# FNet mixing plus a GEGLU feed-forward: where a third seven-product form starts, which hidden block keeps its left sums, and when weights are asked for

## The chip, the cores and the metric

The kernel runs on one core of one Trainium2 chip. The metric is the device time of one execution in microseconds (us). Before the change three runs gave 1032.2, 1033.59 and 1035.08 us; the median is 1033.59 us. The profile comes from one more execution, with a time of its own (see below).

## The reference, cut to what matters

```python
# x: 2048 x 640; w_gate, w_up: 640 x 1728; w_down: 1728 x 640; all fp32
g = sigmoid((x * gate_w).sum(-1, keepdims=True))
a = x @ dft_hid_re ; b = x @ dft_hid_im           # DFT along the hidden side
y = dft_seq_re @ a - dft_seq_im @ b               # DFT along the sequence, real part
h = gelu(x @ w_gate) * (x @ w_up)                 # 2048 x 1728, tanh form
out = g * y + (1 - g) * (h @ w_down)
```

The change lies in the first third of the program, where `h` is computed; its last lines touch the first loads of the DFT.

## The kernel before, in words

**Products.** Every fp32 matrix product is made of three TensorE matmuls on reduced-precision parts: each operand is split into a "high" part (a ScalarE copy with rounding, L82) and a "low" part (the rest, a VectorE subtraction, L85), and `mm3` issues high by high (L101), high by low (L102) and low by high (L103). A low part can also be made without VectorE: `negative` writes minus the high part on ScalarE (L93), and `left_of` adds the raw data onto it with an accumulating DMA that GpSimd issues (L97).

**Seven products.** Large products are cut 2 by 2 and computed with seven block products in place of eight, from sums of blocks. On the weight side these sums are S1 to S4 (VectorE, L311 to L317), a difference D (`diff`, L330), and for pairs of blocks sums "across" the pair. On the side of x they are T1 to T4.

**The loop.** The 1728 columns of `h` are done as 13 blocks of 128 and a rest. Blocks 1 to 12 are the loop `for f in range(1, NF)`. From block `PAIRED` = 3 on, two neighbours form a pair: the odd one (kind 1) carries further seven-product forms over both, `together` (names ending in t: `pH7t`) and `together_up` (u). From block `THIRD` on there is a third such form, `together_s`, for S1 times T1 (s). Its weight operands are called `wt`: raw parts `wt9a`, `wt9b` (loaded by `load_third`, L267), their sums (L277, and L280 to L283 across), highs, and lows. Its x operands `xs` are made once, from blocks read back (`loads_s`), with sums at L1298 to L1303 and splits, kept in DRAM, and read again for each pair by `load_across` (GpSimd's DMA queue, L1329); `xq` and `xu` are the same for the other two forms. An even block (kind 2) of such a pair finds S1 times T1 already in its bank, so its group of S1 is missing, and its group of S4 stands in the place of S1.

**A block's matmuls.** `gate_up` issues, for each half tp of the rows, products into the banks X and Z: A11, S1 (or S4), then S2 (`xT02`, `xT12` with `ws..`), D, S3, S4, and a last small one into X with `u5` (`x05`, `x15` with `wa`). VectorE empties X between them: L637 adds X to a sum after A11 and before S2 may write X, L675 after S3 and before `u5`, L691 after `u5`; L667 takes Z after D in an even block of a pair with `together_s`. In the other blocks S4 into Z stands between S3 and `u5`. ScalarE copies a bank at L149. A matmul that writes X again waits for the one that emptied it. In an odd block L587 empties the bank `pH7s` in `together_s`.

**Left sums.** For the hidden blocks k listed in `STORED` (k counts pairs of f: k=1 is f=3 and 4, k=2 is f=5 and 6), the sums that the later product with `w_down` needs on its left side are made right here (L700 in the odd block, `last_sums` after the even one) and written to DRAM. For the k that is not listed they are made later.

**Order.** Within `in_order` the engines TensorE, ScalarE, VectorE and GpSimd run exactly in the order in which the code issues. The loop interleaves by `fills`, a queue of small pieces with a cost in units of VectorE time: after each group of matmuls `fill(ns)` issues as many pieces as the share of the block's matmul time allows. `make_w(f + 1)` gives the pieces that prepare the next block's weights, `make_third(f + 2)` those of `wt`, `make_up` those of `wu`. Raw weights are asked for on SyncE's queue: `load_w` takes `wa..r` (512 KB), `wb`, and for odd blocks `wq..r`. Tiles of 4 KB per partition share 46 slots, so a load can wait until the last reader of the slot's old tile is done.

**After the loop** the DFT follows: it has its own groups `pL`, `pX`, `pZ`, `pV` from operands `ch`/`cl` (DFT matrix) and `xah`/`xal` (x). Its first x operands, `split_xa(0)` to `split_xa(2)`, are made in block 12. Then come the products with `w_down` in an order of k, and the last sums.

Of the kernel before, what the change touches and what calls it, by code (L numbers as in the profile page):

```python
# [22 lines left out]
NF = F // P  # L23
# [1 line left out]
NK = (NF - 1) // 2  # L25
GM_AT = [5, 19]
EORD = [0, 2, 1, 3, 4]
STORED = (0, 2, 3)
PAIRED = 3
THIRD = 5  # L30
XB_AT = [0, 1, 2, 3, 4, 5, 9, 11]
WU_AT = [17, 19, 33, 35, 50]
HL_AT = [21, 37]
# [4 lines left out]
def kernel(  # L38
# [167 lines left out]
    def pair_of(f):  # L206


        return 0 if f < PAIRED or f >= NF else 2 - (f - PAIRED + 1) % 2
# [3 lines left out]
    def load_w(f):  # L213


        if f >= NF:
            return
        ra, rb = slot(F32, [P, 8, P], f"wa{f}r"), wsmall(F32, f"wb{f}")
        nc.sync.dma_start(ra, wf[f - 1, :, :8])
        nc.sync.dma_start(rb, wf[f - 1, :, 8:])  # L220
        rq = None
        if pair_of(f) == 1:
            rq = slot(F32, [P, 8, P], f"wq{f}r")
            nc.sync.dma_start(rq[:, 0:2], wf[f, :, 0:2])
            nc.sync.dma_start(rq[:, 2], wf[f, :, 4])
        wraw[f] = ra, rb, rq
# [35 lines left out]
    def load_third(f):  # L262

        traw[f] = a, b = [mtile(F32, f"wt{f}{n}").rearrange("p (b c) -> p b c", c=P) for n in "ab"]
        for v, c in ((a, 8), (b, 2)):
            for q in range(2):
                nc.sync.dma_start(v[:, 2 * q : 2 * q + 2], wf[f - q, :, c : c + 2])  # L267
# [30 lines left out]
    def make_w(f):  # L298
# [96 lines left out]
        if kind == 1:  # L395
            if f > PAIRED:
                work = [(0, high_a), (0, neg_a), (84, across), (0, low_a), (56, across2), (0, high_q)]
                work += [(84, sums), (109, low_q), (84, sums2), (0, high_c), (56, diff), (122, low_c)]
            else:
                work = [(84, across), (56, across2), (0, high_a), (0, high_q), (122, low_a), (109, low_q)]  # L400
                work += [(84, sums), (84, sums2), (56, diff)]
                late_work.extend([(0, high_c), (122, low_c)])
        elif kind == 2:
            work = [(84, sums), (28, diff_here), (0, high_a), (84, sums2), (122, low_a), (61, high_c), (0, low_c)]
        else:
            work = [(84, sums), (0, high_a), (84, sums2), (0, high_c), (122, low_a), (56, diff), (122, low_c)]
# [705 lines left out]
    W0, load_part, parts, first_strassen = load_first()  # L1112
    Bs = []
    B, tiles, load, piece, tsum, his, lows = load_x(0)
# [28 lines left out]
    with in_order(ACT, DVE, PE):  # L1143
# [48 lines left out]
        B, tiles, load, piece, tsum, his, lows = load_x(1)  # L1192
# [62 lines left out]
        W, work = make_w(1)  # L1255
        sums, high_a, sums2, high_c, low_a, diff, low_c = (do for _, do in work)
# [70 lines left out]
    def load_across(f, n, to, kept, k):  # L1327
        v = slot(F32R, [P, 2, T], f"{n}{f}{k}")
        nc.gpsimd.dma_start(v.bitcast(F32), kept[k - 1])  # L1329
        to[f"T{k}"] = v[:, 0], v[:, 1]  # L1330

    fills, state = deque(), {}
# [27 lines left out]
    with in_order(PE, ACT, DVE, POOL):  # L1360
        for f in range(1, NF):
# [6 lines left out]
            if kind == 1:  # L1368
                up, work = make_up(f, load_up(f))
# [6 lines left out]
            third = kind == 1 and f >= THIRD  # L1376
            if f + 1 < NF and not third:
                nxt, work = make_w(f + 1)
                if pair_of(f + 1) == 1 and f + 1 >= THIRD:
                    ws, (sums, across, highs, lows) = make_third(f + 1)  # L1380
                    work = [sums, *work[:2], across, *work[2:4], highs, work[4], lows, *work[5:]]
                if kind != 1 or f == PAIRED:
                    fills.extend(work)
            if kind == 1 and PAIRED < f < THIRD:
                fills.extend(work)
            if f == NF - 1:
                for k in range(2):
                    fetch_xn(k)
                    load_c(k)

                def made():
                    sums_made.pop(0)()

                for k in range(2):
                    fills.extend([(126, partial(split_xa, k)), (122, made), (245, partial(split_c, k))])
                fills.extend([(126, partial(split_xa, 2)), (122, made)])
            state.update(pe=0, done=0, all=sum(c for c, _ in fills), pe_all=2450 if not kind else (2994, 1768)[kind - 1] if f < THIRD else (3198, 1496)[kind - 1])
            s5 = pair(F32, f"s5{f}")
            xs = {}
            work = [gate_up(f, W, Bs[tp], tp, s5[:, tp], s1t, xs, s4, zs) for tp in range(2)]  # L1400
# [11 lines left out]
            for k in range(4):  # L1412
                run(more)
                if third and k in (1, 3):
                    load_across(f, "xs", Ts, kepts, k)
            for step in range(8 if not kind else 7):
                if third and step == 5:
                    unpark(f + 1, zs, parks)
# [35 lines left out]
                    fills.extend(s123[:3])  # L1454
                if f == THIRD - 1 and step == 5:
                    todo.extend(s4th)
                if step == 5 and THIRD <= f + 2 < NF and pair_of(f + 2) == 1:
                    load_third(f + 2)
                if third and step == 1:
                    load_w(f + 1)  # L1460
                    nxt, parts = make_w(f + 1)
                    fills.extend(parts)
                    state["all"] += sum(c for c, _ in parts)
                if step == 5 and not (f + 2 >= THIRD and pair_of(f + 2) == 2):
# [461 lines left out]
```

## Time and profile before

| what | us |
|---|---|
| median of three runs | 1033.59 |
| the profiled execution | 1031.1 |
| its span, first to last instruction | 1029.3 |
| TensorE busy / VectorE / ScalarE / GpSimd | 1014.8 / 837.2 / 511.8 / 188.9 |
| loop blocks 3 to 12 (first matmul of block 3 to the first stretch of pure DFT) | about 93 to 360 |

The first matmuls of the blocks, read from the timeline of TensorE, stand at 93.25 (f=3), 123.96, 143.76, 176.13 (f=6), 193.75, 227.53 (f=8), 245.08, 279.21 (f=10), 295.49 and 327.68 us (f=12). In what follows E8 is the first matmul of block 8, and E8+9.8 means 9.8 us behind it.

How to read it: a row of the timeline has start, duration, engine, line, operation, output<-inputs, shapes, and in brackets how long the engine stood idle just before and which instruction released it. A row of the waits has the engine and line that waited, what it waited for, the sum, the number of waits and the longest. TensorE starts matmuls of 512 columns every 0.23 us though each shows as 0.39 us, since they overlap.

### The profile page before, as it was taken

Reading aid. Unit: us, or ns where it says so; the run is one execution under the profiler, and the core shown is the slowest. Engines: PE = TensorE matmul, PEld = TensorE weight load, DVE = VectorE, ACT = ScalarE, POOL = GpSimd, SP = SyncE. Lnnn points to the kernel's source line nnn. Section 1 sums busy time; section 2 is a strip of 40 time slices with the busy share of each in tenths; the row PEclk is TensorE's granted clock in tenths of the full one; section 3 lists DMA queues with packets and bytes.
Section 4 is the critical chain, followed back from the end, with each engine's and each line's share of the span. In section 5 each row is a group of like instructions: output and inputs, shape, how many; then the busy total and the mean of one; then the engine's idle time right before and its main releaser. Section 6 shows DMA issues by size and latency. Waiting matters only on the chain.

```text
span 1029.3 us, 13418 instructions
## 1 busy us (share of the span) xinstructions
PE 1014.8 (99%) x4477; PEld 832.8 (81%) x4477; DVE 837.2 (81%) x1197; ACT 511.8 (50%) x666; POOL 188.9 (18%) x330
## 2 busy tenths in 40 slices
PE   9999999999999999999999999999999999999998
PEld 7888778777778788888888888888888888888887
DVE  7887786868666798986977797779798997997796
ACT  6644455454545484533444444434627737665340
POOL 1221240414130010032104301320111010111112
PEclk9999999999999999999999999999999999999999
DMA  9566684757586897589669966979989999997856
GB/s 350 156 212 225 208 276 176 248 209 254 197 268 228 269 265 225 199 300 388 232 201 341 376 220 218 375 267 325 328 306 384 353 395 335 344 364 216 269 147 98
DMA packets 98598, 276.51 MB, mean 269 GB/s; under 512 B 13088, under 2 KB 25504, under 8 KB 98528
## 3 DMA queue, kind: packets, MB, share of 16 engines
q1 hardware_dynamic: 69216, 182.88, 51.1%
q0 software_dynamic: 29024, 92.57, 28.2%
q8 instruction: 35, 0.57, 0.2%
q14 instruction: 35, 0.29, 0.1%
q10 hardware_dynamic: 288, 0.20, 0.1%
HBM read 201.13 MB, written 66.60 MB: 260 GB/s over the span
## 4 chain that ended last, share of the span: by engine, by line
PE 81%; issue 10%; DVE 4%; POOL 3%; DMA 1%; ACT 0%; POOLq 0%; SPq 0%; DVEq 0%; ACTq 0%
PE pX L102 5%; PE pX L103 5%; PE pX L101 5%; PE pL L103 3%; PE pL L102 3%; PE pL L101 3%; PE pZ L103 3%; PE pZ L101 3%; PE pZ L102 3%; PE pV L103 2%; PE pV L102 2%; PE pV L101 2%; PE pY L103 1%; PE pR L103 1%; PE pQ L103 1%
## 5 line engine op out<-in xcount | busy, mean ns | idle before, releaser
L82 ACT ACTIVATE ch<-csa 128x1024 fp32r<-128x1024 f32 x32 | 34.0, 1063 | 79.6 <-DVE csa L894 66.8
L456 POOL DMA_DIRECT2D hA<-s x48 | 26.2, 546 | 165.8 <-DVE s L687 145.4
L82 ACT ACTIVATE ch<-cra 128x1024 fp32r<-128x1024 f32 x32 | 33.9, 1060 | 45.2 <-DVE cl L85 14.2
L85 DVE TENSOR_TENSOR cl<-cra,ch 128x1024 fp32r<-128x1024 f32 x32 | 39.1, 1221 | 19.7 <-ACT ch L82 16.2
L85 DVE TENSOR_TENSOR cl<-crb,ch 128x1024 fp32r<-128x1024 f32 x32 | 39.1, 1221 | 13.3 <-ACT ch L82 13.1
L102 PE MATMUL pL<-cl,xah 128*128 128x512 f32 x128 | 49.8, 389 | 0.0
L103 PE MATMUL pL<-ch,xal 128*128 128x512 f32 x128 | 49.8, 389 | 0.0
L101 PE MATMUL pL<-ch,xah 128*128 128x512 f32 x128 | 48.7, 389 | 0.0
L82 ACT ACTIVATE ch<-crb 128x1024 fp32r<-128x1024 f32 x32 | 33.8, 1056 | 27.0 <-DVE cl L85 9.7
L85 DVE TENSOR_TENSOR cl<-csa,ch 128x1024 fp32r<-128x1024 f32 x32 | 39.1, 1221 | 9.9 <-ACT ch L82 8.8
L149 ACT ACTIVATE s<-pX 128x512 f32<-128x512 f32 x41 | 24.1, 596 | 37.4 <-PE pX L103 36.8
L85 DVE TENSOR_TENSOR cl<-csb,ch 128x1024 fp32r<-128x1024 f32 x32 | 39.2, 1224 | 4.2 <-ACT ch L82 3.2
L82 ACT ACTIVATE ch<-csb 128x1024 fp32r<-128x1024 f32 x32 | 34.0, 1061 | 12.5 <-DVE csb L897 4.3
L1526 POOL DMA_DIRECT2D uA<-c x8 | 4.3, 540 | 168.5 <-DVE c L1638 168.3
L102 PEld LDWEIGHTS pL<-cl,xah 128*128 128x128 f32 x128 | 24.0, 188 | 5.0
L103 PEld LDWEIGHTS pL<-ch,xal 128*128 128x128 f32 x128 | 24.0, 188 | 5.0
L101 PEld LDWEIGHTS pL<-ch,xah 128*128 128x128 f32 x128 | 24.0, 188 | 5.0
L82 ACT ACTIVATE kh<-kw 128x1024 fp32r<-128x1024 f32 x24 | 25.5, 1062 | 5.1 <-PE kL L102 4.2
L675 DVE TENSOR_TENSOR s<-s,pX 128x512 f32<-128x512 f32 x24 | 16.1, 682 | 13.0 <-PE pX L103 13.0
L102 PE MATMUL pX<-cl,xah 128*128 128x512 f32 x64 | 25.0, 391 | 0.7 <-DVE cl L85 0.7
L85 DVE TENSOR_TENSOR kl<-kw,kh 128x1024 fp32r<-128x1024 f32 x18 | 21.9, 1218 | 4.4 <-ACT kh L82 4.4
L681 ACT ACTIVATE s<-s 128x512 f32<-128x512 f32 x16 | 10.1, 634 | 30.3 <-DVE s L680 30.3
(3785 smaller groups left out, 3524.8 us busy)
## 6 DMA issues: line engine op xcount, KB each, us to landing
cra<-in_ct SPq DMA_DIRECT2D x64, 512.0 KB, 5.1
crb<-in_ct SPq DMA_DIRECT2D x64, 512.0 KB, 5.8
kr<-hA SPq DMA_DIRECT2D x36, 512.0 KB, 7.7
hA<-s POOLq DMA_DIRECT2D x48, 256.0 KB, 3.1
ux<-uA SPq DMA_DIRECT2D x24, 512.0 KB, 8.0
ux<-uT SPq DMA_DIRECT2D x16, 512.0 KB, 6.5
hT<-s POOLq DMA_DIRECT2D x24, 256.0 KB, 5.3
xq<-xp POOLq DMA_DIRECT2D x12, 512.0 KB, 5.3
```

The source lines that it names most:

```text
L82: nc.scalar.activation(hi, raw, AF.Copy)
L85: nc.vector.tensor_tensor(lo, raw, hi.bitcast(F32), op=ALU.subtract)
L101: nc.tensor.matmul(ps, lh, rh, start=first, stop=False, skip_group_check=True)
L102: nc.tensor.matmul(ps, lh, rl, start=False, stop=False, skip_group_check=True)
L103: nc.tensor.matmul(ps, ll, rh, start=False, stop=last, skip_group_check=True)
L149: nc.scalar.activation(m, src, AF.Copy)
L456: nc.gpsimd.dma_start(to[:, i], src)
L675: tt(s5, s5, X, op=ALU.add)
L681: nc.scalar.activation(s2, s2, AF.Gelu_apprx_tanh)
L1526: nc.gpsimd.dma_start(to[:, i], src)
```

## The change

1. `THIRD` goes from 5 to 7: the pair of blocks 5 and 6 computes S1 times T1 in the plain way, and only the pairs 7/8, 9/10 and 11/12 use `together_s`. The sums of `xs` across, which were made in blocks 3 and 4, are made in blocks 5 and 6. TensorE issues 4496 instructions of matmul in place of 4493.
2. `STORED` goes from (0, 2, 3) to (0, 1, 3): the left sums are made at once for blocks 3 and 4 and no longer for 5 and 6. After the loop k=1 and k=2 change places.
3. In an odd block from `THIRD` on, `load_w` of the next block and `load_third` of the next pair are issued after the third step of `together`, where `load_w` stood at step 1 and `load_third` at step 5 of the even block. The pieces of `make_third(f + 2)` move from the even block into the odd one, among the next block's pieces.
4. For odd blocks above 3 the pieces of `make_w` get a new order: the difference D's sum and high part ahead of the high part of the sums S, its low part ahead of the low part of the sums.
5. In block 12 `split_xa(1)` and `split_xa(2)` make their lows by ScalarE's `negative` and the accumulating DMA. Only `split_xa(0)` still uses VectorE's subtraction.

```diff
@@ -25,9 +25,9 @@
 NK = (NF - 1) // 2
 GM_AT = [5, 19]
 EORD = [0, 2, 1, 3, 4]
-STORED = (0, 2, 3)
+STORED = (0, 1, 3)
 PAIRED = 3
-THIRD = 5
+THIRD = 7
 XB_AT = [0, 1, 2, 3, 4, 5, 9, 11]
 WU_AT = [17, 19, 33, 35, 50]
 HL_AT = [21, 37]
@@ -395,7 +395,7 @@
         if kind == 1:
             if f > PAIRED:
                 work = [(0, high_a), (0, neg_a), (84, across), (0, low_a), (56, across2), (0, high_q)]
-                work += [(84, sums), (109, low_q), (84, sums2), (0, high_c), (56, diff), (122, low_c)]
+                work += [(84, sums), (109, low_q), (84, sums2), (28, diff_high), (0, high_c), (28, diff_low), (122, low_c)]
             else:
                 work = [(84, across), (56, across2), (0, high_a), (0, high_q), (122, low_a), (109, low_q)]
                 work += [(84, sums), (84, sums2), (56, diff)]
@@ -1376,7 +1376,7 @@
             third = kind == 1 and f >= THIRD
             if f + 1 < NF and not third:
                 nxt, work = make_w(f + 1)
-                if pair_of(f + 1) == 1 and f + 1 >= THIRD:
+                if f + 1 == THIRD:
                     ws, (sums, across, highs, lows) = make_third(f + 1)
                     work = [sums, *work[:2], across, *work[2:4], highs, work[4], lows, *work[5:]]
                 if kind != 1 or f == PAIRED:
@@ -1392,8 +1392,8 @@
                     sums_made.pop(0)()
 
                 for k in range(2):
-                    fills.extend([(126, partial(split_xa, k)), (122, made), (245, partial(split_c, k))])
-                fills.extend([(126, partial(split_xa, 2)), (122, made)])
+                    fills.extend([(126, partial(split_xa, k, not k)), (122, made), (245, partial(split_c, k))])
+                fills.extend([(126, partial(split_xa, 2, False)), (0, made)])
             state.update(pe=0, done=0, all=sum(c for c, _ in fills), pe_all=2450 if not kind else (2994, 1768)[kind - 1] if f < THIRD else (3198, 1496)[kind - 1])
             s5 = pair(F32, f"s5{f}")
             xs = {}
@@ -1413,6 +1413,10 @@
                 run(more)
                 if third and k in (1, 3):
                     load_across(f, "xs", Ts, kepts, k)
+                if third and k == 2:
+                    load_w(f + 1)
+                    if f + 2 < NF:
+                        load_third(f + 2)
             for step in range(8 if not kind else 7):
                 if third and step == 5:
                     unpark(f + 1, zs, parks)
@@ -1454,11 +1458,13 @@
                     fills.extend(s123[:3])
                 if f == THIRD - 1 and step == 5:
                     todo.extend(s4th)
-                if step == 5 and THIRD <= f + 2 < NF and pair_of(f + 2) == 1:
+                if step == 5 and f + 2 == THIRD:
                     load_third(f + 2)
                 if third and step == 1:
-                    load_w(f + 1)
                     nxt, parts = make_w(f + 1)
+                    if f + 2 < NF:
+                        ws, (sums, across, highs, lows) = make_third(f + 2)
+                        parts = [*parts[:3], sums, across, *parts[3:5], highs, parts[5], lows, *parts[6:]]
                     fills.extend(parts)
                     state["all"] += sum(c for c, _ in parts)
                 if step == 5 and not (f + 2 >= THIRD and pair_of(f + 2) == 2):
```

**Blocks 3 and 4 on VectorE**, from the sums of block 3's last products to the instruction that empties X in block 4 (L637). `s_..` are sums of 512 columns. Before:

```order
L1302 TENSOR_TENSOR xs_1217<-xs_1217,xst_1227 128x512
L1303 TENSOR_TENSOR xs_1219<-xs_1219,xs_1217 128x512
L680 TENSOR_TENSOR s_1_1146<-s_1_1146,pZ_1_1052 128x512
L687 TENSOR_TENSOR s_0_1134<-s_0_1134,s_1001 128x512
L691 TENSOR_TENSOR s_1179<-s_1179,pX_0_1042 128x512
L692 TENSOR_TENSOR s_1033<-s_1033,s_1179 128x512
L687 TENSOR_TENSOR s_1_1146<-s_1_1146,s_1001 128x512
L691 TENSOR_TENSOR s_1196<-s_1196,pX_1_1051 128x512
L692 TENSOR_TENSOR s_1040<-s_1040,s_1196 128x512
L85 TENSOR_TENSOR xs_1297<-xs_1217,xs_1297 128x512
L85 TENSOR_TENSOR xs_1303<-xs_1215,xs_1302 128x512
L637 TENSOR_TENSOR s_1124<-s_1124,pX_0_1289 128x512
```
Now:

```order
L680 TENSOR_TENSOR s_1_1146<-s_1_1146,pZ_1_1052 128x512
L687 TENSOR_TENSOR s_0_1134<-s_0_1134,s_1001 128x512
L691 TENSOR_TENSOR s_1179<-s_1179,pX_0_1042 128x512
L692 TENSOR_TENSOR s_1033<-s_1033,s_1179 128x512
L700 TENSOR_TENSOR s_1001<-s_0_1134,s_1033 128x512
L687 TENSOR_TENSOR s_1_1146<-s_1_1146,s_1001 128x512
L691 TENSOR_TENSOR s_1196<-s_1196,pX_1_1051 128x512
L692 TENSOR_TENSOR s_1040<-s_1040,s_1196 128x512
L700 TENSOR_TENSOR s_1001<-s_1_1146,s_1040 128x512
L637 TENSOR_TENSOR s_1124<-s_1124,pX_0_1266 128x512
```

Four rows on `xs` (L1302, L1303 and two splits, L85) are gone from here, as are three more just ahead of it (L1298, L1299 and a split), and two L700 have come. The seven `xs` rows now stand at the same place of blocks 5 and 6, ahead of block 6's L637.

**Block 7 on VectorE**, around the low part of `wu7` and L587, which empties `pH7s`. `ws8r` are the sums for block 8, `wt9a` and `wt9b` the parts for the third form of block 9. Before:

```order
L85 TENSOR_TENSOR wu7l<-wu7r,wu7h 128x640
L311 TENSOR_TENSOR ws8r<-wb_1977,wa8r 128x256
L312 TENSOR_TENSOR ws8r<-wa8r,wb_1977 128x256
L587 TENSOR_TENSOR sz_1972<-sz_1972,pH7s 128x512
L343 TENSOR_TENSOR wa8r<-wa8r 128x128
L316 TENSOR_TENSOR ws8r<-ws8r,wa8r 128x256
L317 TENSOR_TENSOR ws8r<-wa8r,ws8r 128x256
L596 TENSOR_TENSOR sz_1942<-sz_1942,pH7s 128x512
```
Now:

```order
L85 TENSOR_TENSOR wu7l<-wu7r,wu7h 128x640
L311 TENSOR_TENSOR ws8r<-wb_1874,wa8r 128x256
L312 TENSOR_TENSOR ws8r<-wa8r,wb_1874 128x256
L343 TENSOR_TENSOR wa8r<-wa8r 128x128
L277 TENSOR_TENSOR wt9a<-wt9a,wt9b 128x512
L280 TENSOR_TENSOR wt9b<-wt9a 128x128
L281 TENSOR_TENSOR wt9b<-wt9a 128x128
L282 TENSOR_TENSOR wt9b<-wt9b,wt9a 128x128
L283 TENSOR_TENSOR wt9b<-wt9a,wt9b 128x128
L316 TENSOR_TENSOR ws8r<-ws8r,wa8r 128x256
L317 TENSOR_TENSOR ws8r<-wa8r,ws8r 128x256
L587 TENSOR_TENSOR sz_1956<-sz_1956,pH7s 128x512
```

L343, the five sums of `wt9`, L316 and L317 now stand between `wu7l` and L587; before, only L311 and L312 did. A little ahead of this piece L242 to L245, the sums of `wu7`, now stand in front of L515, L520 and L521; before, they stood behind L521 and L714.

**Block 8 on ScalarE**, where the weights of block 9 get their high parts (`wd` is D, `ws9h` the sums, `wq9h` those across the pair). Before:

```order
L82 ACTIVATE wq9h<-wq9r 128x896
L149 ACTIVATE s_0_2216<-pX_0_2160 128x512
L149 ACTIVATE s_1_2226<-pX_1_2176 128x512
L82 ACTIVATE ws9h<-ws9r 128x1024
L82 ACTIVATE wd_2234<-wb_2118 128x128
L668 ACTIVATE s_0_2216<-s_0_2216 128x512
L671 ACTIVATE s_1967<-s_1967 128x512
```
Now:

```order
L82 ACTIVATE wq9h<-wq9r 128x896
L149 ACTIVATE s_0_2186<-pX_0_2140 128x512
L82 ACTIVATE wd_2194<-wb_2098 128x128
L149 ACTIVATE s_1_2197<-pX_1_2151 128x512
L82 ACTIVATE ws9h<-ws9r 128x1024
L668 ACTIVATE s_0_2186<-s_0_2186 128x512
L671 ACTIVATE s_1951<-s_1951 128x512
```

`wd` has moved from behind `ws9h` to the place between the two copies of X (L149); `ws9h` stays behind the second copy.

## The prediction

> **What bounds the kernel now.** I read the page first, then the waits of TensorE, then the timeline at each of those waits.
>
> ```profile
> PE 1014.8 (99%) x4477; PEld 832.8 (81%) x4477; DVE 837.2 (81%) x1197; ACT 511.8 (50%) x666; POOL 188.9 (18%) x330
> ```
> ```profile
> PE pX L101 <- DVE s L675: 4.4, 3, 1.7
> PE pX L101 <- DVE s L637: 2.2, 3, 1.6
> PE pH9s L101 <- DVE sz L587: 1.6, 1, 1.6
> PE pH7s L101 <- DVE sz L587: 1.3, 1, 1.3
> PE idle L1147 <- PEq L1914: 0.8, 1, 0.8
> PE pX L102 <- DVE cl L85: 0.7, 1, 0.7
> ```
> ```profile
> 360.00:1029.00 669.00, 666.22 (x2965) 550.71 (x2963) 567.72 (x730) 326.60 (x371) 107.50 (x180) 1.00 0.85 287
> ```
>
> TensorE is the bound: 99% busy, clock 1.00. The row of the windows (columns: stretch, length, busy time and count of TensorE, weight loads, VectorE, ScalarE, GpSimd, clock, DMA share, GB/s) shows that behind 360 us it never rests for long: 669 us for 2965 matmuls is 0.226 us each. So a microsecond won in the loop arrives at the end as it is. What there is to win is the list of waits without the idle warm-up row: 4.4+2.2+1.6+1.3+0.7 = 10.2 us in 9 waits. Each is followed by a matmul that takes 0.50 in place of 0.39 us (row 132.48 below), so I count 0.1 more for each: 11.1 us. Every one lies between 124 and 360 us, and every one waits for VectorE.
>
> **The change part by part.** *Extra matmuls.* Three more at 0.226 us: +0.7 us, sure.
>
> *Block 4.* L637 empties X, and S2 waits for it.
>
> ```profile
> 123.56 0.69 DVE L85 TENSOR_TENSOR xs<-xst,xs 128x512 fp32r<-128x512 f32 x1 [1.22 <-ACT xs L82]
> ...
> 130.54 1.28 DVE L85 TENSOR_TENSOR xs<-xs,xs 128x512 fp32r<-128x512 f32 x2
> 131.74 0.68 DVE L637 TENSOR_TENSOR s<-s,pX 128x512 f32<-128x512 f32 x1
> ```
> ```profile
> 132.48 0.50 PE L101 MATMUL pX<-xT02h,ws4h 128*128 128x512 f32 x1 [1.56 <-DVE s L637]
> ```
>
> Ahead of it go seven `xs` instructions at 0.60 us from start to start (two in 130.54 to 131.74), 4.2 us, and the wait of 1.22; two L700 come, at about 0.65: −4.1 us. L637 was 1.6 late, so it is early: the wait is gone: −1.6.
>
> *Block 6* gets these rows in its turn. Its L637 was late by 0.3 (2.2 − 1.56 − 0.3 for block 8). New ahead of it: four of the seven, 2.4 (the other three fall into block 5). Gone: two L700 (1.3) and, since they move behind it, `wt7`'s five sums and three small ones of `wq7`, which is only partly a gain, as VectorE waited there for nothing but its own row. Counted out row by row I get L637 ending 7.7 us behind E6 where TensorE wants it at 6.8: a wait of 1.0. Bounds: 0.3 as it was, 1.6 as in block 4; I take 1.0. On the other hand L675 no longer matters there: with S1 done in the plain way, S4 (twelve matmuls, 2.7 us) stands between S3 and the one that waits, and its 1.7 us go. Sum −1.0.
>
> *Blocks 8 and 10.* The late one is L675:
>
> ```profile
> 237.85 0.60 ACT L149 ACTIVATE s<-pX 128x512 f32<-128x512 f32 x1 [0.67 <-PE pX L103]
> 239.01 1.06 ACT L82 ACTIVATE ws9h<-ws9r 128x1024 fp32r<-128x1024 f32 x1 [0.56 <-DVE ws9r L317]
> ```
> ```profile
> 240.30 0.29 DVE L85 TENSOR_TENSOR wd<-wb,wd 128x128 fp32r<-128x128 f32 x1 [1.12 <-ACT wd L82]
> 240.51 0.68 DVE L667 TENSOR_TENSOR s<-s,pZ 128x512 f32<-128x512 f32 x1
> 241.11 1.22 DVE L85 TENSOR_TENSOR ws9l<-ws9r,ws9h 128x1024 fp32r<-128x1024 f32 x1
> 242.24 0.68 DVE L667 TENSOR_TENSOR s<-s,pZ 128x512 f32<-128x512 f32 x1
> 242.84 1.27 DVE L675 TENSOR_TENSOR s<-s,pX 128x512 f32<-128x512 f32 x2
> ```
> ```profile
> 243.57 0.50 PE L101 MATMUL pX<-x05h,wa 128*128 128x512 f32 x1 [1.68 <-DVE s L675]
> ```
>
> The wait of 1.12 for `wd` goes (ScalarE makes its high part behind `ws9h`, from now on ahead of it), and the sums of the next third form, 2.2 us, have left this block. That would be 3.3 us on VectorE, twice what is missing. But `ws9h` stays behind the second copy on ScalarE, and that copy waits for TensorE (0.67). So now ScalarE sets the time: the copy at 237.4 (0.4 sooner, as L637's waits in this block go), `ws9h` from 238.0 to 239.0, `ws9l` to 240.2, two L667 to 241.4, L675 to 242.0, where TensorE wants it at 241.3 (243.57 less the 1.68 and the slow matmul gives 241.7, less 0.4). A wait of 0.7 stays (bounds 0 and 1.7). So −1.0 here, −0.3 for L637, and −0.3 in block 10, whose wait was 1.0 (4.4 − 1.7 − 1.7) and is limited in the same way.
>
> *Blocks 7 and 9.*
>
> ```profile
> 210.28 0.82 DVE L85 TENSOR_TENSOR wu7l<-wu7r,wu7h 128x640 fp32r<-128x640 f32 x1 [3.07 <-ACT wu7h L82]
> 213.71 0.43 DVE L311 TENSOR_TENSOR ws8r<-wb,wa8r 128x256 f32<-128x256 f32 x1 [2.60 <-DMA wa8r<-in_wf]
> ...
> 214.38 0.68 DVE L587 TENSOR_TENSOR sz<-sz,pH7s 128x512 f32<-128x512 f32 x1
> ```
>
> In block 7 the raw weights come late; asked for at the block's start they end the wait of 2.60. In exchange L343, the five sums of `wt9`, L316 and L317 go ahead of L587: 0.2 + 0.6 + 4 × 0.2 + 0.8 = 2.4 us. And the sums of `wu7` now stand ahead of three instructions of 0.60 us (L515, L520, L521), which fill part of the wait of 3.07 for `wu7h`: I put `wu7l` 1.2 us sooner. L587 then comes 2.6 + 1.2 − 2.4 = 1.4 sooner, and it was 1.3 late; since two of the three are estimates I count 0.3 left (bounds 0 and 1.3). In block 9 the third form's sums fall behind L587, so its 1.6 goes whole. Sum −2.6.
>
> *Block 12.* The two lows leave VectorE for ScalarE and an accumulating DMA.
>
> ```profile
> 339.19 1.06 ACT L82 ACTIVATE xah<-xn 128x1024 fp32r<-128x1024 f32 x1 [3.92 <-DVE xn L860]
> ```
> ```profile
> L93 ACT ACTIVATE xal<-xn x5: 1042/1044/1048, 358.5 to 380.7; 128x1024 fp32r<-128x1024 f32 x5
> L97 POOL DMA_DIRECT2D xal<-xn x5: 857/874/895, 360.0 to 382.2; - x5
> ...
> DMA to landing us min/median/max: 6.1/7.3/9.3
> ```
> ```profile
> 346.32 0.39 PE L103 MATMUL pX<-ch,xal 128*128 128x512 f32 x1
> ```
> ```profile
> 359.05 0.50 PE L102 MATMUL pX<-cl,xah 128*128 128x512 f32 x1 [0.73 <-DVE cl L85]
> ```
>
> The negative starts at 340.2, the DMA 1.5 us later (358.5 to 360.0) at 341.6, and lands by the row at 347.7 to 350.9. TensorE read this low at 346.32; its order now puts the reading five matmuls later, at 347.4. At the lower end the wait is 0.3, at the median 1.5, at the upper end 3.5. DMA is less busy there than at the rows' own time, so I take 0.4. The second low, by the order alone, is asked for some 7 us before TensorE reads it: hidden by the two lower landings, late by 2.3 by the upper; I take 0. In return VectorE is free of two lows of 1.2 us and their waits, and the 0.7 at 359.05 shrinks to 0.2. Sum −0.1.
>
> The sums of k=1 and the swap of k behind the loop I cost at nothing:
>
> ```profile
> 144.00:176.00 32.00, 32.00 (x141) 26.10 (x140) 18.86 (x34) 16.83 (x30) 4.92 (x10) 1.00 0.59 209
> ...
> 194.00:227.50 33.50, 32.20 (x141) 26.18 (x140) 20.57 (x36) 15.81 (x27) 8.14 (x16) 1.00 0.73 251
> ```
>
> In block 5 (first row) VectorE has 13 of 32 us free and TensorE waits for nothing. Six sums and the three `xs` rows fit there; without that cover the six are 3.6 us.
>
> **Sum:** +0.7 −1.6 −1.0 −1.0 −0.3 −0.3 −2.6 −0.1 = −6.2, and with six waits in place of nine three slow matmuls fewer, −0.3: **−6.5 us**, 1024.6 against the profiled 1031.1. The median of the three runs is 2.5 above the profiled one, so the same gain reads 1027 there; I predict 1025.5, between.
>
> **A rule that speaks against it.** The earlier loads (1 MB: `wa` 512 KB and the raw third form 512 KB) run beside the reading of `xs`:
>
> ```profile
> 199.95 1.18 POOL L1329 DMA_DIRECT2D xs<-xs  x2 [1.02 <-DMA xs<-xs]
> ```
> ```profile
> DMA to landing us min/median/max: 6.3/6.6/6.9
> ```
> ```profile
> 206.75 0.39 PE L101 MATMUL pZ<-xs,wt7h 128*128 128x512 f32 x1
> ```
> ```profile
> 299.78 0.33 SPq L219 DMA_DIRECT2D wa12r<-in_wf  x1
> ```
> ```profile
> DMA to landing us min/median/max: 6.6/6.9/7.1
> ```
>
> The first landing line belongs to the two rows of block 7, with no weights beside them, the last to those of block 11 at 299.5, with `wa12r` beside them: 0.3 us longer. The Trainium skill, DMA: Bandwidth & Descriptors, section Issuing engines are not separate DMA queues, says that transfers of all issuing engines share the same 16 DMA engines and interleave. By that rule 1 MB ahead would cost `xs` all of its own time; the two landing lines show little of it.
>
> **Rivals.** *Waits that only move* (15%): L587 with more ahead of it stays at 1.3, block 6 takes 1.6, blocks 8 and 10 keep 1.7 and 1.0. That is 1.0 + 0.6 + 1.3 = 2.9 more: 1028.4. For it: each place is an order written out, with margins under 1 us. Against: the 2.60 and 1.12 are waits for a load and a copy that plainly move.
>
> *The loads come no sooner* (10%): `wa8r` needs a slot, whose last reader is a late matmul of block 6. If VectorE still gets it only at 213.7, the 2.4 us put ahead of L587 come on top: 1.3 grows to 3.7 in block 7 (0.3 counted), and block 9 keeps its 1.6. That is 5.0 more: 1030.5.
>
> *Transfers come late* (8%, slower): `xs` at 199.95 lands at 206.3 and is read at 206.75, a margin of 0.5; in block 9 I put it at 0.5 too, an estimate, once the stalls ahead are gone. 1 MB at block 7's 251 GB/s is 4.2 us; all of it ahead of `xs` costs 3.7 twice, and `xal` landing at 9.3 costs 3.1 more than I count: 10.5 more, or 1036. It decides at `xs` landings of 8.5 us with `xal` at 9.3: then 3.1 and twice 1.7 eat the gain of 6.5; at 10.1 it is slower by more than 3.1. Against: 7.1 was the longest `xs` beside a weight load.
>
> **How the numbers follow.** Forecast 67%, rivals 15, 10 and 8%. Bounds: all waits gone (3.3 counted as left, and six slow matmuls) gives 1021.6, a little less with the small gaps that the view of the waits leaves out; the second rival at the median's level 1033. Range 1020.5 to 1033.5. A difference under 0.3% (3.1 us) can't be told from none: faster takes the forecast and most of the first rival, 0.79; same the second and the rest, 0.13; slower 0.08.
>
> **What would show it.** Right: no wait for L637 in block 4 but one in block 6 near 1.0; no `DVE ws8r <- DMA wa8r` among VectorE's waits; L675 twice near 0.7, behind `ws9h`; no wait of `pH9s` for L587; 4496 matmuls' worth of work. Wrong: TensorE waiting for a DMA of `xs`, `xq` or `xal`, or for L587 with more than 1 us.

## The result, and the profile after

| | before | after |
|---|---|---|
| median of four runs, us | 1033.22 | 1028.22 |
| lowest to highest, us | 1032.2 to 1035.08 | 1027.82 to 1028.87 |
| profiled execution, us | 1031.1 | 1028.07 |
| its span, us | 1029.3 | 1026.3 |

The ratio is 0.995, with a 95% interval of 0.9933 to 0.9967: about 0.5% or 5.0 us by the medians, 3.0 us between the two profiled executions. The prediction said 1025.5 in a range of 1020.5 to 1033.5, so the sign is as forecast and the time lies inside the range, 2.7 us above the number named. Of 58 more runs of the kernel before, 25 show a mean granted clock of 1.000, with a median of 1032.06 us, and 33 one of 0.998 or less, with 1034.09; the profiled execution of before (1.000) is of the first kind and all four runs of the changed kernel (0.998) are of the second, so the 3.0 us do not compare like with like, and against the second kind the gain is 5.9 us by the medians.

The page of the changed kernel, and its waits of TensorE:

```profile
span 1026.3 us, 13389 instructions
...
PE 1015.4 (99%) x4480; PEld 835.0 (81%) x4480; DVE 832.0 (81%) x1186; ACT 508.8 (50%) x660; POOL 188.6 (18%) x329
```
```profile
PE pX L103 <- DMA xal<-xn: 2.2, 1, 2.2
PE pX L101 <- DVE s L675: 1.3, 2, 0.7
PE pX L101 <- DVE s L637: 1.0, 1, 1.0
PE pZ L101 <- ACT s L149: 1.0, 1, 1.0
PE pZ L101 <- DMA xs<-xs: 0.9, 1, 0.9
PE idle L1147 <- PEq L1920: 0.8, 1, 0.8
```

The page of before has 4477 matmuls, this one 4480: three more, as said, though the text ahead of the prediction has 4493 and 4496. Without the last row of the waits these are 6.4 us in six waits, where there were 10.2 in nine. The reader should compare the list with that of before by what TensorE waits for. Then it was VectorE in every row. Now VectorE has 2.3 us, at the places and of the sizes forecast: L637 in block 6, L675 in blocks 8 and 10. Waits for L587 in blocks 7 and 9 are gone, as is the one for `cl` at the seam. The other 4.1 us are new and are waits for transfers. Two are for `xs`; the row that names ScalarE's L149 is of the same kind, since the matmul that waited there reads `xs`:

```profile
254.04 0.47 PE L101 MATMUL pZ<-xs,wt9h 128*128 128x512 f32 x1 [1.00 <-ACT s L149]
```

That `xs` was issued at 245.18 and landed after 8.7 us, at 253.9, just ahead of the matmul. The third transfer is the low of an x operand of the DFT.

That last one costs more than its row. The timeline of TensorE there (start, duration, idle time before), and its windows (last columns: clock, DMA share, GB/s):

```profile
361.21 0.50 PE L103 MATMUL pX<-ch,xal 128*128 128x512 f32 x1 [2.18 <-DMA xal<-xn]
...
362.53 0.63 PE L102 MATMUL pL<-cl,xah 128*128 128x512 f32 x1
362.96 0.63 PE L103 MATMUL pL<-ch,xal 128*128 128x512 f32 x1
...
365.89 0.39 PE L102 MATMUL pV<-cl,xah 128*128 128x512 f32 x1
```
```profile
355.00:360.00 5.00, 4.03 (x18) 3.00 (x16) 4.47 (x7) 4.79 (x5) 0.89 (x1) 1.00 1.04 305
...
366.00:368.00 2.00, 2.00 (x11) 1.62 (x10) 2.00 (x3) 1.96 (x3) 0.00 (x0) 1.00 0.99 209
```
```profile
362.40:365.80 3.40, 3.40 (x10) 2.62 (x9) 2.87 (x5) 2.94 (x4) 0.87 (x1) 0.50 1.03 346
```

About a microsecond behind the wait the granted clock falls to 0.50 for 3.4 us. Matmuls start every 0.43 us (362.53 to 362.96) in place of 0.23: seven of them, and two in part, make 1.5 us more. So this single wait costs 3.7 us.

Take all intervals between matmul starts that are longer than 0.3 us, from 90 to 372 us, and add up what each has beyond the usual 0.227 us: 14.4 us before and 10.9 us after, −3.5. With three matmuls more, +0.7, that is −2.8 of the −3.0 in the span.

### The profile page after: what moved, and what is told of

Its sections match the earlier page's. It is cut to its first block, busy times and chain, and to the rows that moved or that the text cites. A ratio compares the mean times of both kernels' runs of the same rounds, so it can differ in the third digit from the quotient of the medians.

```text
span 1026.3 us, 13389 instructions
## 1 busy us (share of the span) xinstructions
PE 1015.4 (99%) x4480; PEld 835.0 (81%) x4480; DVE 832.0 (81%) x1186; ACT 508.8 (50%) x660; POOL 188.6 (18%) x329
## 4 chain that ended last, share of the span: by engine, by line
PE 91%; DVE 3%; DMA 3%; issue 2%; ACT 1%; POOL 0%; DVEq 0%; POOLq 0%; ACTq 0%
PE pX L103 6%; PE pX L101 6%; PE pX L102 6%; PE pZ L101 4%; PE pZ L102 4%; PE pZ L103 4%; PE pL L103 3%; PE pL L102 3%; PE pL L101 3%; PE pV L101 2%; PE pV L102 2%; PE pV L103 2%; PE pR L102 1%; PE pQ L102 1%; PE pY L102 1%
## 5 line engine op out<-in xcount | busy, mean ns | idle before, releaser
L85 DVE TENSOR_TENSOR cl<-cra,ch 128x1024 fp32r<-128x1024 f32 x32 | 39.1, 1222 | 24.0 <-ACT ch L82 21.8
L85 DVE TENSOR_TENSOR cl<-crb,ch 128x1024 fp32r<-128x1024 f32 x32 | 39.1, 1222 | 16.1 <-ACT ch L82 14.7
L85 DVE TENSOR_TENSOR cl<-csa,ch 128x1024 fp32r<-128x1024 f32 x32 | 39.1, 1221 | 8.4 <-ACT ch L82 6.2
L149 ACT ACTIVATE s<-pX 128x512 f32<-128x512 f32 x41 | 24.1, 596 | 40.9 <-PE pX L103 40.0
L85 DVE TENSOR_TENSOR cl<-csb,ch 128x1024 fp32r<-128x1024 f32 x32 | 39.2, 1224 | 4.2 <-ACT ch L82 3.2
L103 PE MATMUL pX<-ch,xal 128*128 128x512 f32 x64 | 25.1, 393 | 2.2 <-DMA xal<-xn 2.2
L85 DVE TENSOR_TENSOR kl<-kw,kh 128x1024 fp32r<-128x1024 f32 x18 | 21.9, 1219 | 4.4 <-ACT kh L82 4.4
L103 PE MATMUL pZ<-ch,xal 128*128 128x512 f32 x64 | 25.4, 397 | 0.0
```

What stands on the lines that cost most here:

```text
L85: nc.vector.tensor_tensor(lo, raw, hi.bitcast(F32), op=ALU.subtract)
L103: nc.tensor.matmul(ps, ll, rh, start=False, stop=last, skip_group_check=True)
L149: nc.scalar.activation(m, src, AF.Copy)
```

## The experiments

Twelve kernels were run, each with runs of the kernel before on the same chip; those had medians of 1033.06 to 1033.54 us. The edits are shown against the changed kernel, or against the one named.

### Why the fourth x operand is late

Theory T was that transfers crowd each other, W that the start of the DFT is a wall. First, the two added accumulating DMAs were taken out:

```diff
-                    fills.extend([(126, partial(split_xa, k, not k)), (122, made), (245, partial(split_c, k))])
-                fills.extend([(126, partial(split_xa, 2, False)), (0, made)])
+                    fills.extend([(126, partial(split_xa, k)), (122, made), (245, partial(split_c, k))])
+                fills.extend([(126, partial(split_xa, 2)), (122, made)])
```

> The changed kernel, but all three first x operands of the DFT get their lows by VectorE's subtraction again, so two accumulating DMAs less. Theory T (transfers): the gain that is missing went into transfers that land late; the low of the fourth x operand (xal, wait of 2.2 us near 361) is late because the two added accumulating DMAs share the engines with it and with the DFT's loads. Then that wait falls below 0.5 us, the slow matmuls behind it (about 1.7 us at granted clock 0.55 to 0.60) go, the wait of TensorE for cl at the seam comes back with 0.7 to 1.3 us, and the time is about 1028.2 - 3.9 + 1.0 = 1025.3 us. Rival W (wall): the start of the DFT is bound by its own stream of loads, so whatever comes sooner in the loop is waited for there: the wait near 361 stays between 1.7 and 2.7 us (for xal or for the DFT matrix) and the time stays within 1 us of 1028.2.

Measured: 1025.47 us (1024.81 to 1026.36), ratio 0.9925 (0.9902 to 0.9948). None of its runs overlaps those of the changed kernel. Its waits of TensorE:

```profile
PE pZ L101 <- DMA xs<-xs: 1.3, 2, 0.8
PE pX L101 <- DVE s L675: 1.3, 2, 0.7
PE pX L101 <- DVE s L637: 1.0, 1, 1.0
PE idle L1147 <- PEq L1920: 0.8, 1, 0.8
PE pX L102 <- DVE cl L85: 0.7, 1, 0.7
```

The wait for `xal` is gone, the old 0.7 for `cl` is back, and the clock does not fall in the loop or at the seam. T's number was 1025.3. The same stretch of 345 to 361 us in the windows of before, of the changed kernel and of this run:

```profile
345.00:361.00 16.00, 15.27 (x66) 12.00 (x65) 11.77 (x19) 8.59 (x11) 3.06 (x5) 1.00 0.73 232
```
```profile
345.00:361.00 16.00, 14.03 (x62) 11.07 (x60) 14.70 (x24) 11.09 (x12) 4.30 (x7) 1.00 1.02 302
```
```profile
345.00:361.00 16.00, 15.27 (x65) 11.75 (x64) 13.56 (x21) 10.62 (x12) 3.91 (x6) 1.00 0.87 252
```

The DMA share is 0.73, 1.02 and 0.87. In the changed kernel the DMA engines are busy all through the stretch, and the low of the fourth operand, issued at 351.81, takes 9.4 us:

```profile
351.81 0.89 POOL L97 DMA_DIRECT2D xal<-xn  x1 [2.76 <-ACT xal L93]
```
```profile
DMA to landing us min/median/max: 9.4/9.4/9.4
```

Before, the same transfer took 6.1 us, and in every run with the lows back on VectorE 5.5 to 6.5. In the three runs that keep the two added DMAs and this one (the changed kernel, store_k2, weights_behind_xs) it took 9.3 to 9.9. The two added lows themselves were in time (5.5 and 6.8 us); the one behind them paid. They did not overlap with it: the second had landed at 351.2, and while the fourth operand's low is under way the share is 1.04 in all three kernels. The difference is a backlog. Two loads of the DFT matrix, `cra` and `crb`, asked for at 345.93 and 348.22, took 10.7 and 10.3 us, so both were still under way when that low was issued; in lows_on_vector they took 5.9 and 7.7 us. That the two added transfers set off the late one is shown by taking them out; that they did it through these loads is read from one pair of traces.

Then only the late low was moved to VectorE:

```diff
-            split_xa(i + 3, False)
+            split_xa(i + 3, i == 0)
```

> The changed kernel, but the low of the fourth x operand alone (the one waited for near 361) is made by VectorE. T: that wait and the slow matmuls behind it go, 1028.2 - 3.9, with at most 0.5 us of a new wait behind it: 1024.3 to 1024.8 us. W: TensorE waits for something else of the DFT between 355 and 372 (a part of the DFT matrix, cl, or the next xal), 2 us or more in all, and the time stays within 1 us of 1028.2.

Measured: 1025.01 us (1023.69 to 1026.04), ratio 0.9918. The wait is gone with its slow matmuls. A wait of 1.4 for `xal` has come at 352.9, for the third operand. It is one of the two that the change makes by DMA, and took 8.4 us here. T's time, 1024.3 to 1024.8, was nearly met, but W has a small part: in seven of the nine kernels with both lows back on VectorE (lows_on_vector and those made from it, all below), a low is late by 0.2 to 1.4 us at one of the operands from the fourth to the sixth.

### Why xs is late

In the changed kernel the loads of `xs` in block 7 (two, issued at 195.6 and 196.2) landed after

```profile
DMA to landing us min/median/max: 8.9/9.2/9.5
```

where it had been 6.3 to 6.9 before. In block 9 it was 7.9 to 8.7, before 4.7 to 5.9. SyncE had asked for the weights just ahead:

```profile
190.06 0.84 SPq L267 DMA_DIRECT2D wt9a<-in_wf  x2
191.00 1.22 SPq L267 DMA_DIRECT2D wt9b<-in_wf  x2
192.31 0.66 SPq L219 DMA_DIRECT2D wa8r<-in_wf  x1
```
```profile
204.56 0.47 PE L101 MATMUL pZ<-xs,wt7h 128*128 128x512 f32 x1 [0.93 <-DMA xs<-xs]
```

First all of it was put behind `xs`:

```diff
-                if third and k == 2:
-                    load_w(f + 1)
-                    if f + 2 < NF:
-                        load_third(f + 2)
+                if third and k == 3:
+                    load_w(f + 1, nc.gpsimd)
+                    if f + 2 < NF:
+                        load_third(f + 2, nc.gpsimd)
```

> The changed kernel, but in blocks 7, 9 and 11 the next raw weights and the raw third form are asked for on GpSimd's queue, right behind the two loads of xs, and not on SyncE's queue ahead of them. T: xs lands in 6 to 7 us as before the change (8.7 to 9.5 in the changed kernel), TensorE's waits for xs in blocks 7 and 9 (1.2 us each with their slow matmul) go, and nothing else gets late by over 0.5 us: 1028.2 - 2.4 = 1025.8 us, with the wait for xal near 361 still at 2.0 to 2.4. W: the waits for xs go too, but the wait near 361 grows by as much, to about 4.5 us, and the time stays at 1028.2 or rises with more slow matmuls. Third possibility: the weights now land too late for L311 and L587 in blocks 7 and 9 is late by 1 us or more.

Measured: 1030.59 us (1027.1 to 1031.38). `xs` landed sooner than before the change:

```profile
DMA to landing us min/median/max: 5.6/5.9/6.2
```

and both waits for it went, as either theory had it. But the third possibility came true:

```profile
PE pX L103 <- DMA xal<-xn: 2.9, 1, 2.9
PE pH9s L101 <- DVE sz L587: 2.7, 1, 2.7
```

In block 9, L311 stood idle for 3.7 us until, by the profile, a store of hT had landed, and the stores were behind six more DMAs in GpSimd's queue. Both waits slowed the clock. The wait for `xal` grew by 0.7 and not by 2.4, so W has no support here, though L587's wait blurs it.

The other three start from lows_on_vector. One step later for the raw third form:

```diff
-                    if f + 2 < NF:
-                        load_third(f + 2)
...
+                    if f + 2 < NF:
+                        load_third(f + 2)
```

> The kernel of the run lows_on_vector (1025.47 us), but in blocks 7 and 9 the raw third form (512 KB) is asked for one step later, just ahead of its sums, while the raw weights stay where they are. Theory: xs lands late (8.5 us) because 1 MB of raw weights has come ahead of it on the shared engines; with 512 KB less in front xs lands about 1.7 us sooner (512 KB at 300 GB/s), the two waits for xs (0.7 and 0.9 us) go, the sums of the third form still get their data: 1023.8 us. Rival: the weights of 512 KB and the stores hA and hT in front of xs set its landing; the waits for xs fall by less than 0.4 us and the time stays at 1025 to 1026.

Measured: 1024.99 us (1024.58 to 1025.31) against 1025.47: not told apart. It was a weak test, since in block 7 the third form still went out at 193.0 to 195.3, ahead of `xs` at 195.9. No wait for `xs` stands in the list of this profile, but `xs` landed after 7.6 to 8.9 us, hardly sooner, and a later run with the same loads (raw_later_old_diff) waits 1.0 us for it. Behind `xs`, on GpSimd's queue:

```diff
-                    if f + 2 < NF:
-                        load_third(f + 2)
+                if third and k == 3 and f + 2 < NF:
+                    load_third(f + 2, nc.gpsimd)
```

> The kernel of the run lows_on_vector, but in blocks 7 and 9 the raw third form is asked for on GpSimd's queue right behind the two loads of xs. Theory: the same landing of xs, 1.7 us sooner, and the waits for xs go, 1023.8 us, unless GpSimd's queue then holds up xu or the stores: four more DMAs of 0.55 us stand ahead of them (2.2 us), and VectorE reuses the stores' tiles, which made L311 3.7 us late in block 9 of weights_behind_xs with six more DMAs. With that, L587 of block 9 is late by up to 1 us: 1024.8 us. Rival as in the run before: the waits for xs fall by less than 0.4 us.

Measured: 1027.53 us (1025.23 to 1029.18). The landing of `xs` in block 7 of this run:

```profile
DMA to landing us min/median/max: 8.5/8.8/9.1
```

With the raw weights still ahead, the raw third form is not what delays `xs`: it is behind now, and nothing has changed. The wait for L587 of block 9 is back with 2.1 us, twice what I had allowed. The whole third part undone:

```diff
-                if third and k == 2:
-                    load_w(f + 1)
-                    if f + 2 < NF:
-                        load_third(f + 2)
...
                 if third and step == 1:
+                    load_w(f + 1)
                     nxt, parts = make_w(f + 1)
-                    if f + 2 < NF:
-                        ws, (sums, across, highs, lows) = make_third(f + 2)
-                        parts = [*parts[:3], sums, across, *parts[3:5], highs, parts[5], lows, *parts[6:]]
```

(and `make_third` and `load_third` as in the kernel before)

> The kernel of the run lows_on_vector with the third part of the change undone: the raw weights asked for at step 1, the raw third form in the even block, its sums made in the even block. Theory: VectorE waits for the weights of block 8 again, L587 is late by about 1.5 us in blocks 7 and 9, L637 of block 8 by 0.3 to 0.5, and L675 of blocks 8 and 10 by about 1.0 as now; the waits for xs (1.6 in sum) go. Sum +3.0 +0.4 +0.2 -1.6 = +2.0: 1027.5 us. Rival: asking sooner pays nothing, since what L587 gains xs loses: 1025 to 1026 us.

Measured: 1031.73 us (1029.1 to 1036.05), 6.3 slower than lows_on_vector (4.8 between the profiled executions). Its waits and its `xs`:

```profile
PE pX L101 <- DVE s L675: 4.6, 2, 2.5
PE pX L101 <- DVE s L637: 1.3, 2, 1.0
```
```profile
DMA to landing us min/median/max: 5.4/5.8/6.1
```
```profile
237.18 1.22 DVE L85 TENSOR_TENSOR ws9l<-ws9r,ws9h 128x1024 fp32r<-128x1024 f32 x1 [1.96 <-ACT ws9h L82]
```

No wait for `xs`, as expected, but I had the place of the loss wrong. L587 was nearly in time (0.2), and L675 of blocks 8 and 10 was late by 2.5 and 2.0, the first with the slow clock behind it. With the sums of the third form back in the even block and D's new order, VectorE waits 1.96 us for `ws9h` (last row) and L675 is pushed out. So as long as the fourth part stays, the third part pays by emptying the even block, and the 1.3 us of waits for `xs` in lows_on_vector are worth it. The run undoes the earlier loads and the moved sums together and keeps D's new order, so what each is worth alone was not measured.

Over the runs the first `xs` of block 7 lands in 7.6 to 9.8 us where `wa8r` (512 KB) is asked for ahead of it, and in 5.4 to 6.3 where it is asked for behind (weights_behind_xs, loads_old and the kernel before), wherever the third form stands. Block 9 shows the same without exception: 7.9 to 8.9 us with `wa10r` ahead, 4.7 to 5.5 with it behind. So the raw weights ahead cost `xs` 2 to 3 us. No kernel had the raw third form ahead and the weights behind, so whether it would do the same alone is not shown. In block 7 there is one exception: in third_from_5 (below) `wa8r` was ahead too, landed in 5.2 us itself, and `xs` took 5.6. What else is in flight counts with it; that was not taken further.

### The first, second and fourth part

```diff
-STORED = (0, 1, 3)
+STORED = (0, 2, 3)
```

> The changed kernel, but the left sums are made at once for blocks 5 and 6 again (k=2) in place of 3 and 4 (k=1). If the choice of k matters by VectorE's order, as the prediction had it: two L700 of 0.65 us come back ahead of L637 of block 6, its wait grows from 1.0 to about 2.3, and six DMAs of hT come back into GpSimd's queue ahead of xs in block 7, whose wait of 0.9 grows by 1 to 2 us: 1030.5 us. Rival: the sums fit into free time in either place: within 0.7 us of 1028.2.

Measured: 1029.31 us (1027.31 to 1033.26). The wait for L637 of block 6 was 1.9 (from 1.0), those for `xs` 3.1 (from 1.9), each of the kind expected and somewhat smaller. The time lies between the 1030.5 of the theory and the rival's 0.7 around 1028.2, and its runs overlap with those of the changed kernel; what is shown is the waits.

From lows_on_vector, the third form from block 5 on again:

```diff
-THIRD = 7
+THIRD = 5
```

> The kernel of the run lows_on_vector with the first part of the change undone: the seven-product S1 times T1 from block 5 on, so three matmuls less (-0.7 us), and the xs sums back in blocks 3 and 4, where the two L700 now stand as well. Theory: L637 of block 4 is late by the old 1.6 plus 1.3 for the two L700, 2.9 us, and after so long a wait TensorE runs slowly for 3.4 us (1.7 us more, as after the waits of 2.2 us and longer so far); block 6 loses its wait for L637 (-1.2) and gets one for L675 (+0.8). 1025.5 - 0.7 + 2.9 + 1.7 - 1.2 + 0.8 = 1029.0 us. Rival: block 4 hides them, and three matmuls less show: 1024.8 us.

Measured: 1029.26 us (1027.57 to 1031.44), expected 1029.0. Block 4 in the timeline, and its window:

```profile
134.22 0.50 PE L101 MATMUL pX<-xT02h,ws4h 128*128 128x512 f32 x1 [3.01 <-DVE s L637]
```
```profile
134.00:138.00 4.00, 3.78 (x11) 3.02 (x12) 3.92 (x14) 1.32 (x3) 2.51 (x4) 0.66 0.94 344
```

The wait of 2.9 came with 3.01, and the slow clock behind it. The three matmuls less are lost in it. That the sum met the median is partly luck: this profile, of the slowest of the eight runs (1031.44 us), also has 2.0 us of waits for `xs` (two of them listed under ScalarE's L149) and 1.4 for `xal`, where the kernel it is made from has 1.3 and none. With the sums of k=1 made in blocks 3 and 4 there is no room for those of `xs` there, and with those of k=2 made in blocks 5 and 6 the wait for L637 of block 6 is 1.9 (above): the first two parts belong together.

From lows_on_vector, the old place of D:

```diff
-                work += [(84, sums), (109, low_q), (84, sums2), (28, diff_high), (0, high_c), (28, diff_low), (122, low_c)]
+                work += [(84, sums), (109, low_q), (84, sums2), (0, high_c), (56, diff), (122, low_c)]
```

> The kernel of the run lows_on_vector (1025.47 us) with the fourth part of the change undone: the difference D is made behind the high part of the sums again, in blocks 4, 6, 8 and 10. Theory: VectorE waits for D's high part again (about 1.1 us each), and as ScalarE's second copy of X sets when the sums' high part is made, only part of it reaches L675: its wait of 0.7 in blocks 8 and 10 grows to 1.2 each, 1026.5 us. Rival: ScalarE alone sets L675 and the order of D costs nothing: waits of 0.7 as now, 1025.5 us.

Measured: 1024.77 us (1024.67 to 1024.94), where lows_on_vector had 1025.47 (1024.81 to 1026.36): not told apart. Neither the theory nor the rival: the waits for L675 in blocks 8 and 10 are gone. Of the 1.3 us, 0.6 came back as a wait for `xal`. ScalarE and VectorE in block 8, first of the changed kernel (lows_on_vector has the same order), then of this run:

```profile
233.78 0.60 ACT L149 ACTIVATE s<-pX 128x512 f32<-128x512 f32 x1
234.28 1.05 ACT L82 ACTIVATE ws9h<-ws9r 128x1024 fp32r<-128x1024 f32 x1
```
```profile
235.36 1.22 DVE L85 TENSOR_TENSOR ws9l<-ws9r,ws9h 128x1024 fp32r<-128x1024 f32 x1 [1.38 <-ACT ws9h L82]
```
```profile
233.28 1.06 ACT L82 ACTIVATE ws9h<-ws9r 128x1024 fp32r<-128x1024 f32 x1 [0.19 <-DVE ws9r L317]
...
234.44 0.58 ACT L149 ACTIVATE s<-pX 128x512 f32<-128x512 f32 x1
```
```profile
234.57 0.29 DVE L85 TENSOR_TENSOR wd<-wb,wd 128x128 fp32r<-128x128 f32 x1 [1.12 <-ACT wd L82]
234.78 1.22 DVE L85 TENSOR_TENSOR ws9l<-ws9r,ws9h 128x1024 fp32r<-128x1024 f32 x1
```

`high_c`, which makes `ws9h`, costs 0 in the queue of pieces. Once `fill` has issued a piece it stops ahead of one that costs 0, and takes that first at its next turn. With `diff_high` (28) in between, `high_c` misses one turn: `diff_high` takes it, the second copy of X follows, and `ws9h` starts behind that copy. In the old order it stands ahead of it. VectorE waits 1.12 for `wd` there, as before the change, and still gets `ws9l` 0.6 sooner.

### Versions that might beat both

From third_raw_later, two splits of block 6 behind L637:

```diff
-            if f == THIRD - 1:
-                fills.extend(s123[3:])
...
-                    work = [sums, *work[:2], across, *work[2:4], highs, work[4], lows, *work[5:]]
+                    work = [sums, *work[:2], across, *work[2:4], highs, work[4], lows, *s123[3:], *work[5:]]
```

> The kernel of the run third_raw_later (1024.99 us), but in block 6 the last two splits of xs stand behind L637 and not ahead of it. Theory: L637 of block 6 is late by just these two splits (1.2 us), so its wait of 1.0 goes and nothing else in block 6 gets late, since S4 stands between S3 and the matmul that waits for L675: 1023.9 us. Rival: the weights of block 7 get late by as much, or xs lands late in block 7 since it is kept later: 1025 us or more.

Measured: 1025.87 us (1024.78 to 1027.66): the wait for L637 fell to 0.4, and the time did not follow. From it, the fourth low on VectorE as in third_low_on_vector:

> The kernel of the run xs_splits_later with the low of the fourth x operand made by VectorE as well. Theory: TensorE's waits for xal behind the seam (0 to 1.4 us from run to run) go, and VectorE has room for the 1.14 us there, since its two cl were done 1.5 us before they were read: 0.5 to 1.3 us faster than xs_splits_later, about 1023 us. Rival: VectorE becomes the bound at the start of the DFT, and the wait for cl at the seam of 0.7 repeats itself with the next x operand: no gain, or up to 1 us slower.

Measured: 1026.41 us (1025.0 to 1028.2), no gain; a wait of 1.2 for `xal` stood at the sixth operand, and 2.5 us of waits for `xs` had come (1.0 of it listed under L149). Last, third_raw_later with the old place of D:

> What paid so far in one kernel: the first and second part of the change, the raw weights sooner but the raw third form one step later (third_raw_later), D's place as before the change (old_diff), lows by VectorE (lows_on_vector). If the gains are independent: no wait for L675 in blocks 8 and 10 (0.8 each with the slow matmul, as in old_diff) and at most 0.3 us for xs (as in third_raw_later), so third_raw_later's 1024.99 less 1.6 and with the wait for xal near 366 at 0.8 to 1.4: 1023.4 to 1024.0 us. Rival: TensorE then runs into the DFT's loads that much sooner and the wait for xal grows by as much: 1024.8 us or more.

Measured: 1024.61 us (1023.08 to 1025.43), ratio 0.9915 (0.9899 to 0.993). No wait for L675 or `xal` in its profile, but 1.0 for `xs` where at most 0.3 was expected. The time lies above the 1023.4 to 1024.0 of the theory and just under the rival's 1024.8. It is the fastest median, but lows_on_vector, third_low_on_vector, old_diff, third_raw_later and this one lie within 0.9 us and their ranges overlap in part. By the medians they are 7.6 to 8.9 us faster than before and about 3 us faster than the change as made.

## Why the prediction was right or wrong

- **Bound and place: right.** A microsecond won in the loop reached the end, but for what was lost again at the seam and in `xs`. Two of the signs named for being wrong did come: TensorE waited for `xs` and for `xal`.
- **The level: a choice without a reason.** The sum gave 6.5 us of gain, which from the median is 1027; 1025.5 was put between that and the profile. Some 1.5 of the 2.7 us by which the time is higher come from that choice. The number named was met by lows_on_vector (1025.47), not by the change. The time is near the first rival's 1028.4, but no wait stands at the size that this rival named, so that is a coincidence.
- **Blocks 4 and 6: right.** Forecast waits for L637: none and 1.0; measured none and 1.00. L675 of block 6 is gone.
- **Blocks 8 and 10: right in size, the cause not seen through.** Forecast 0.7 each, measured 0.67 each. I wrote that `ws9h` "stays behind the second copy", as if given. The run old_diff shows that the change's fourth part keeps it there; without that part the thinned VectorE order takes the whole wait away. The row of before could not show this, since there `ws9h` was behind both copies anyway.
- **Blocks 7 and 9: right for L587** (0.3 and 0 forecast; no row for either in the waits). In block 7 of the changed kernel the test is blurred: L587 comes 20.4 us behind the block's first matmul, where it was 20.6, and TensorE is not held up because it has just waited for `xs`. In weights_behind_xs and third_raw_later, without that wait, L587 comes at 19.2, which is the 1.4 sooner of the prediction.
- **Block 12: a step that failed.** I bounded the landing of the two lows that the change makes by DMA and took 0.4; they cost nothing. I did not ask what 512 KB twice does to the transfers behind them: that term was left out of the sum without a reason. The fourth operand's low took 9.4 us for 6.1: 2.2 us of waiting and 1.5 of slow matmuls.
- **The loads ahead of `xs`: the other step that failed.** They were put at nothing, since I took block 11 as proof that weights beside `xs` cost 0.3 us. There `wa12r` was asked for 0.3 us behind the first `xs` and 0.4 ahead of the second, after the loads before them had landed; in block 7 it now went out 3.3 us ahead, among other loads under way, and `xs` took 2.6 us longer, which made waits of 0.9 and 1.0 us. The rule cited from the Trainium skill (DMA: Bandwidth & Descriptors, Issuing engines are not separate DMA queues) was the better guide, and the traces agree with it: issuing from another engine's queue did not protect `xs`. The rival "transfers come late" had the mechanism and a chance of 8%; its price was too high, since the margin of 0.5 us was too small: TensorE wanted `xs` of block 7 some 7.9 us behind its issue, where it had been 6.8, so a landing of 8.9 cost only 0.9.
- **The extra for each wait was too small.** I counted 0.1 us beyond the row. At 238.43 the row says 0.67; from start to start that matmul is 0.83 late, and the next one another 0.11. The other waits for VectorE show the same: some 0.27 beyond the row.
- **The clock was not in the sum at all.** It cost 1.5 us behind the wait for `xal`.

## What to carry to other kernels

Moving a transfer or turning an engine's work into a transfer has to be priced at the transfers that follow it on the shared engines: look for the first one behind with a margin under the added time. A piece that costs nothing in a list of paced work is placed by the rule for its turn, so putting another in front of it can move it past an instruction that waits. And a wait just above 2 us can cost nearly twice its length.

## What the runs showed of the hardware that was not expected

The granted clock fell behind some waits and not behind others. By idle time in the waits of all the profiles: none of the waits up to 1.8 us slowed it; of those of 1.9 to 2.1 us two did (1.9 for `xs` in store_k2, 2.1 for L587 in third_raw_behind_xs) and others did not (1.9 for L637 in store_k2, 2.0 for L675 in loads_old); all from 2.2 to 3.0 us did. Each time the clock stood at 0.50 for 3.4 us and matmuls started every 0.43 us, 1.4 to 1.6 us in all. The drop does not begin at a fixed place: in loads_old it began 0.4 us before the wait ended, in the changed kernel 1.2 us behind it. The Trainium skill, TensorE: Matmul & The Clock Gate, section Why this matters for your kernels, names idle gaps of more than about 3 us as the ones to avoid; here shorter ones were enough, and the measurement decides.
